# Twenty-four copies of memory values and four copies of keys: from VectorE to ScalarE

## The chip, the cores and the metric

The kernel runs on one core of one Trainium2 chip. The metric is the time of one execution on the device, in microseconds (us). Three runs of the kernel before gave 243.59, 243.83 and 243.85 us; their median is 243.83 us. Engines are named as in the profile: PE is TensorE, ACT is ScalarE, DVE is VectorE, POOL is GpSimd, SP is the queue that issues most stores and transposing DMAs.

## What is computed

The program is a chunked attention with a short context, followed by a gated feed-forward layer:

```python
# q, k, v: (4, 8, 768, 64); mem_k, mem_v: (4, 8, 8, 64)
for c in range(24):                       # chunks of 32 queries
    l, r = max(0, 32*c - 16), min(768, 32*c + 40)
    k_full = concat([mem_k, k[:, :, l:r]], axis=2)
    v_full = concat([mem_v, v[:, :, l:r]], axis=2)
    a = softmax(q[:, :, 32*c:32*c+32] @ k_full.T / 8)
    out[:, :, 32*c:32*c+32] = a @ v_full
x = out.transpose(0, 2, 1, 3).reshape(3072, 512)
y = (relu(x @ w_gate) * (x @ w_val)) @ w_out      # w_gate, w_val: 512x1536, w_out: 1536x512
```

Eight memory rows stand ahead of the context of every chunk, in the keys and in the values. They belong to a batch and a head, so all 24 chunks of a batch and head use the same eight rows.

## The kernel before

**Tiles and stages.** The 3072 rows are 24 tiles of 128 rows, six to a batch (`TPB`); a tile holds four chunks. For each tile `a` the attention stage runs: transposes of queries and keys, copies of them to `qT` and `kT`, `scores` (L283, into `s_ps`), `row_max` and `subtract` on DVE, `exponent` on ACT (three ACTIVATEs, L323), `row_sum`, `reciprocal` and `normalise` on DVE (`p_n`, L338), a transpose of the weights (`pT`, L344, by DMA from tile 14 on), then `values` (L354, 32 products into `xT_ps`, from tile 18 on `values_q`) and a copy to `xT`. The feed-forward stage works on blocks of 3, 3, 3, 4, 3, 4 and 4 tiles. For each of twelve column groups `m` PE makes `g_ps` and `v_ps` (four matmuls each, L407), ACT takes the relu of `g_ps` (L413), DVE multiplies it with `v_ps` (L419), and when all twelve are done, `second` (L428) makes `out_ps`, twelve matmuls for a tile, which ACT copies to `o_sb` (L90).

**Buffers that tie the engines together.** `g_ps`, `v_ps` and `out_ps` share four PSUM buffers (pool `fps`, L82). The transposes of queries, keys and weights and the results of `values` share two (`aps`, L84), and there is one for the scores (`sps`). The values lie in two sets `v_bd` (L106): a batch `b` uses set `b % 2`, so batch 2 writes over batch 0, and batch 3 over batch 1.

**The memory rows.** `mem_rows(b, par, hp, eng)` (L153 to L161) writes the eight memory rows of one head pair `hp` and one parity `par` to all 24 chunks of the set: 8 partitions of 24*64 = 1536 values, from an SBUF tile `vmem`, read with a step of 0 over the chunks. A batch takes eight such copies. Batch 0 gets its rows in another way (`pattern_spread`, L175), so there are 24 copies, for batches 1 to 3. `values` of the first tile of a batch needs all eight of its batch (L549).

**The memory keys.** `mem_keys(b, eng)` (L246) copies the keys of the memory to all chunks of `kT`: one copy of 128 partitions x 768 values for each batch. From tile 15 on, the keys are transposed by DMA to a tile `k_t` in SBUF, and `qk_copy` (L271) moves them into `kT`, 128 x 512 values.

**What sets the order.** The program writes its instructions in an order that a list scheduler in the kernel finds when the program is built (`schedule`, L673 to L781). Each operation is entered with `op(key, {engine: cost}, function, deps, prio, ...)`. An operation with two engines in its list goes to the one that is free first when it is ready: so do the copies of `pT`, `xT` and most of `qT` and `kT`. Whenever an engine falls free, the scheduler gives it the ready operation with the lowest `prio`: relu and gate have (0, ...), the copies to `o_sb` (0.5, ...), the attention stages of tile `a` (1, a, ...), the memory rows (1.5,), and `g_ps`, `v_ps` and `out_ps` on PE (2, ...). Nothing is interrupted once it has begun. On the chip each engine then runs its own list in that order. `holds_port` (L669) marks copies that, when DVE does them, the scheduler makes wait for POOL's current instruction; the marked ones are those of this change and a few others.

The rows of batch 1 may be copied once `vmem` has come and the scores of tile 6 have been started; those of batch 2 once `values` of tile 5 is done and the scores of tile 8 have been started; those of batch 3 after `values` of tile 11 and the scores of tile 14 (`MEM_LEAD`, L60 and L633). POOL issues the loads of queries, keys, values and weights in the order of `LOADS` (L63); SP issues stores and the transposing DMAs. Neither queue gets an instruction more or less by the change.

Of the kernel before, what the change touches and what calls it, by code (L numbers as in the profile page):

```python
# [15 lines left out]
ACT = mybir.ActivationFunctionType  # L16
# [4 lines left out]
def kernel(  # L21
# [12 lines left out]
    nc = tc.nc  # L34
# [53 lines left out]
    def copy(eng, o, i):  # L88
        if eng is nc.scalar:
            nc.scalar.copy(o, i)  # L90
        else:
            eng.tensor_copy(o, i)
# [60 lines left out]
    def mem_rows(b, par, hp, eng):  # L153
        p = slice(64 * par, 64 * par + NMEM)
        src = vmem[p, b, HP * par + hp]
        i = bass.AP(tensor=src.tensor, offset=src.offset, ap=[src.ap[0], [0, NCH], [1, D]])
        o = v_bd[b % NSET][p, hp, :, D * par:D * par + D]
        if eng is nc.sync:
            eng.dma_start(o, i)
        else:  # L160
            eng.tensor_copy(o, i)  # L161

    def pattern_load():
        for par in range(2):
# [56 lines left out]
    def pair_t(r, i):  # L221
        ps = TMP["pair", r, i] = aps.tile([128, 2, HP, 128], BF16, tag="aps", name="qk_ps")
        x = qk_b.pop(("pair", r, i))
        for j in range(2):
            for hp in range(HP):
                for r in range(2):
                    nc.tensor.transpose(ps[D * r:D * r + D, j, hp, :], x[:, 2 * hp + r, j, :], ident_b)  # L227

    def pair_q_copy(r, eng):
        b, t = divmod(2 * r, TPB)  # L230
        copy(eng, qT[b][:, :, 128 * t:128 * t + 256].rearrange("p h (s j) -> p j h s", j=2), TMP.pop(("pair", r, 0)))

    def pair_k_copy(r, j, eng):
        b, t = divmod(2 * r, TPB)
        ps = TMP["pair", r, 1]
        o = kT[b][:, :, 4 * t:4 * t + 8, :]
        copy(eng,
             bass.AP(tensor=o.tensor, offset=o.offset + j,
                     ap=[o.ap[0], [NCH * KW, HP], [KW, 8], [16 + NMEM, 2], [2, 8]]),
             ps[:, j].rearrange("p h (c x s) -> p h c x s", c=8, x=2))  # L240

    def new_batch(b):
        qT[b] = kvpool.tile([128, HP, S], BF16, name="qT")
        kT[b] = kvpool.tile([128, HP, NCH, KW], BF16, name="kT")

    def mem_keys(b, eng):  # L246
        src = kmemT[:, b]
        copy(
            eng, kT[b][:, :, :, 16:16 + NMEM],
            bass.AP(tensor=src.tensor, offset=src.offset,  # L250
                    ap=[src.ap[0], [NMEM, HP], [0, NCH], [1, NMEM]]))
# [4 lines left out]
    def qk_t(a, i):  # L256
        ps = TMP["qk", a, i] = aps.tile([128, HP, 128], BF16, tag="aps", name="qk_ps")
        x = qk_b.pop((a, i))
        for hp in range(HP):
            nc.tensor.transpose(ps[:, hp, :], x[:, 2 * hp:2 * hp + 2, :].rearrange("p h d -> p (h d)"), ident_b)  # L260

    def qk_dma(a, i):
        b, t = divmod(a, TPB)
        x = qk_b.pop((a, i)).rearrange("p h d -> p (h d)")
        if i == 0:
            o = qT[b][:, :, 128 * t:128 * t + 128]
        else:
            o = TMP["qk", a, i] = ktpool.tile([128, HP, 128], BF16, name="k_t")
        nc.sync.dma_start_transpose(o, x)

    def qk_copy(a, i, eng):  # L271
        b, t = divmod(a, TPB)
        ps = TMP.pop(("qk", a, i))
        if i == 0:
            copy(eng, qT[b][:, :, 128 * t:128 * t + 128], ps)
        else:
            o = kT[b][:, :, 4 * t:4 * t + 4, :]
            copy(eng,
                 bass.AP(tensor=o.tensor, offset=o.offset,
                         ap=[o.ap[0], [NCH * KW, HP], [KW, 4], [16 + NMEM, 2], [1, 16]]),  # L280
                 ps.rearrange("p h (c x s) -> p h c x s", c=4, x=2))
# [168 lines left out]
    def op(key, eng, fn, deps=(), prio=(0,), take=(), give=(), after=()):  # L450
        ops[key] = dict(eng=eng, fn=fn, deps=list(deps), prio=prio, take=list(take), give=list(give),
                        after=list(after))
# [4 lines left out]
    def psum(n):  # L457
        return {"ACT": 0.07 + 0.83e-3 * n, "DVE": 0.08 + 1.04e-3 * n}

    engine = {"ACT": nc.scalar, "DVE": nc.vector}  # L460
# [20 lines left out]
    for b in range(B):  # L481
        op(("kv", b), {"PE": 0.01}, lambda e, b=b: new_batch(b), take=["kv"],
           prio=(-5.5,) if b == 0 else (1, TPB * b - 2, 0), after=[("t", TPB * b - 2, 0)] if b else [])
        op(("new", b), {"DVE": 0.35, "ACT": 0.75}, lambda e, b=b: mem_keys(b, engine[e]), ["kmc", ("kv", b)],
           prio=(-4.5,) if b == 0 else (1, TPB * b - 2, 0))


    def pace(a):
        blk = block_of[a]
        if starts[blk] < TPB:  # L490
            return []
        m = NDC * (blk - 1) + NDC * (a - starts[blk]) // BLOCKS[blk] - LEAD[blk]
        return [("f", *divmod(max(m, 0), NDC), 0)]
# [4 lines left out]
    for a in range(NT):  # L498
        b, t = divmod(a, TPB)
        last = t == TPB - 1  # L500
        for i in (1, 0):
            if a < 2 * PAIRS:
                if a % 2:
                    continue
                op(("t", a, i), {"PE": 0.57}, lambda e, a=a, i=i: pair_t(a // 2, i), [("qk2", a // 2, i), "ib", ("kv", b)],
                   (1, a - i, 0), ["aps"], ["pr"], pace(max(a - i, 0)))
                if i:
                    for j in range(2):
                        op(("tc", a + j, i), {"ACT": 0.64, "DVE": 0.64}, lambda e, a=a, j=j: pair_k_copy(a // 2, j, engine[e]),
                           [("tc", a, i) if j else ("t", a, i)], (1, a - i, j), (), ["aps"] * j)  # L510
                else:
                    op(("tc", a, i), {"ACT": 1.2, "DVE": 1.22}, lambda e, a=a: pair_q_copy(a // 2, engine[e]), [("t", a, i)],
                       (1, a, 0), (), ["aps"])
            elif a < BY_DMA[i]:
                op(("t", a, i), {"PE": 0.24}, lambda e, a=a, i=i: qk_t(a, i), [("qk", a, i), "ib", ("kv", b)],
                   (1, a - i, 0), ["aps"], ["qk"], pace(max(a - i, 0)))
                op(("tc", a, i), psum(HP * 128), lambda e, a=a, i=i: qk_copy(a, i, engine[e]), [("t", a, i)],
                   (1, a - i, 0), (), ["aps"])
            else:
                op(("t", a, i), {"SP": 1.3}, lambda e, a=a, i=i: qk_dma(a, i), [("qk", a, i), ("kv", b)],  # L520
                   (1, a - i, 0), ["kt"] * i, ["qk"], [("p", a - i - 4)])
                if i:
                    op(("tc", a, i), {"ACT": 0.5, "DVE": 0.28}, lambda e, a=a, i=i: qk_copy(a, i, engine[e]),
                       [("t", a, i)], (1, a - i, 0), (), ["kt"], [("s", a - 2)] + pace(a - 1))
                else:
                    op(("tc", a, i), {"PE": 0.01}, lambda e: None, [("t", a, i)], (1, a - i, 0))
# [77 lines left out]
    def load_v_op(b, half, par, c0, c1, n, deps, after):  # L604
        for i, part in enumerate(reversed(v_parts(b, par, c0, c1))):
            rows = part[3] - part[2]
            load(("vl", b, half, n) if i == 0 else ("vx", b, n), rows * (part[5] - part[4]),
                 rows * (part[5] - part[4]) * 1.15e-3, lambda part=part: load_v_rows(*part), deps, (), after)
# [15 lines left out]
    def load_batch(b):  # L624
        deps = [("z", x) for x in range(HP)] if b < NSET else [("v", TPB * (b - NSET + 1) - 1)]
        for par in range(2):
            for hp in range(HP):
                if b <= MEM_BY_SP:
                    op(("mr", b, par, hp), {"SP": 0.73}, lambda e, b=b, par=par, hp=hp: mem_rows(b, par, hp, nc.sync),
                       deps + [(("vm", par), 0.2)], (0, par, hp))  # L630
                else:
                    op(("mr", b, par, hp), {"DVE": 0.48}, lambda e, b=b, par=par, hp=hp: mem_rows(b, par, hp, nc.vector),
                       deps + [("vm", par)], (1.5,), (), (), [("s", TPB * b - MEM_LEAD[b])])  # L633
        for par in range(2):
            load_v_op(b, 0, par, 0, HP * NCH, par, [], deps)
# [179 lines left out]
```

## Time and profile before

| | us |
|---|---|
| median of three runs | 243.83 |
| the profiled execution's own time | 244.88 |
| span of its records | 243.1 |
| PE busy | 228.5 |
| DVE busy | 146.4 |
| ACT busy | 114.7 |
| POOL busy | 77.9 |

The granted clock of TensorE is full in all 40 slices of the span. The span holds the records of the engines and their DMAs; 1.78 us of the profiled execution lie around it, and the profiled execution is 1.05 us above the median. The share of a row is an average over the whole span: the start (to about 27 us) has the first batch's attention, the stretch from 27 to 65 us has the products of the first two blocks, with attention of tiles 6 to 8 between them, from 65 to 86 us PE makes the `out_ps` of those two blocks, and from 86 us on block follows block. From 200 us on there is no attention left.

Matmuls of a chain overlap: four of `g_ps` for a three-tile block show 0.81 us, and the next chain of four begins 0.65 us after them.

### The profile page before, as it was taken

What the parts mean: (1) busy time and instruction counts of PE and PEld (TensorE: products, weight loads), DVE (VectorE), ACT (ScalarE), POOL (GpSimd) and SP (SyncE); (2) the same over time, 40 slices, a digit from 0 to 9 for tenths busy, and PEclk for the clock granted to TensorE, in tenths of its full rate; (3) what the DMA queues carried; (4) which work ended last, traced back from release to release, by engine and by line L of the source; (5) the groups of instructions that cost most, each with busy time, mean ns of one, the idle gap of its engine ahead of it and who ended that gap; (6) DMA issues with size and microseconds to landing.
All of it is one profiled execution on the core that took longest, in us unless ns stands there. A gap on an engine that the chain in (4) does not pass through costs nothing.

```text
span 243.1 us, 6045 instructions
## 1 busy us (share of the span) xinstructions
PE 228.5 (94%) x2521; PEld 123.7 (51%) x2521; DVE 146.4 (60%) x264; ACT 114.7 (47%) x239; POOL 77.9 (32%) x88
## 2 busy tenths in 40 slices
PE   0889899999997999999999999999999999999995
PEld 0667565655642565555444545665444444444443
DVE  5499963577899527984679428865258851143400
ACT  3658634556633365656545336554245532333212
POOL 8997899975347540428010000000000000000000
PEclk9999999999999999999999999999999999999999
DMA  6999999999999999989999332852421233200022
GB/s 65 175 153 173 166 164 181 199 187 171 147 138 214 201 175 135 139 71 101 124 196 117 65 108 71 128 103 51 131 67 22 27 61 110 88 2 0 0 81 94
DMA packets 114876, 27.97 MB, mean 115 GB/s; under 512 B 106016, under 2 KB 111904, under 8 KB 114848
## 3 DMA queue, kind: packets, MB, share of 16 engines
q0 software_dynamic: 91840, 16.61, 88.0%
q1 hardware_dynamic: 23008, 10.97, 21.0%
q8 instruction: 20, 0.33, 0.6%
q14 instruction: 8, 0.07, 0.1%
HBM read 33.24 MB, written 6.29 MB: 163 GB/s over the span
## 4 chain that ended last, share of the span: by engine, by line
PE 86%; DVE 8%; DMA 2%; ACT 1%; issue 1%; SPq 1%; ACTq 0%; DVEq 0%
PE g_ps L407 26%; PE v_ps L407 26%; PE out_ps L428 22%; PE qk_ps L227 3%; PE xT_ps L361 2%; DVE v_bd L161 2%; PE s_ps L295 2%; DMA kmem_f<-in_mem_k_dram 2%; PE pT_ps L344 1%; DVE p_n L338 1%; DVE sm L327 1%; DVE dif L315 1%; DVE mx L308 1%; PE idle_ps L399 1%; PE x_ps L371 1%
## 5 line engine op out<-in xcount | busy, mean ns | idle before, releaser
L419 DVE TENSOR_TENSOR gvT<-v_ps,g_relu 128x384 f16<-128x384 f32 (+1 forms) x84 | 51.4, 612 | 55.9 <-PE v_ps L407 55.0
L407 PE MATMUL g_ps<-xT,w_gate_sb 128*128 128x384 f16 (+1 forms) x336 | 76.2, 349 | 0.6 <-issue 0.5
L407 PE MATMUL v_ps<-xT,w_val_sb 128*128 128x384 f16 (+1 forms) x336 | 76.1, 349 | 0.0
L413 ACT ACTIVATE g_relu<-g_ps 128x384 f16<-128x384 f32 (+1 forms) x84 | 45.0, 536 | 58.9 <-PE g_ps L407 44.6
L428 PE MATMUL out_ps<-w_out_sb,gvT 128*128 128x512 f16 (+2 forms) x300 | 65.7, 371 | 0.0
L407 PEld LDWEIGHTS <-w_gate_sb 128*128 128x128 f16 x336 | 31.8, 98 | 28.7 <-issue 1.1
L407 PEld LDWEIGHTS <-w_val_sb 128*128 128x128 f16 x336 | 31.5, 98 | 27.6
L428 PEld LDWEIGHTS <-gvT 128*128 128x128 f16 x300 | 27.7, 98 | 29.8
L185 POOL DMA_DIRECT2D v_bd<-in_v_dram x24 | 27.4, 1150 | 9.7 <-issue 5.5
L90 ACT COPY o_sb<-out_ps 128x512 f32<-128x512 f32 (+2 forms) x25 | 14.2, 567 | 32.0 <-PE out_ps L428 29.9
L323 ACT ACTIVATE p_exp<-dif 128x64 f16<-128x64 f32 (+2 forms) x72 | 19.5, 335 | 11.1 <-DVE dif L315 10.9
L308 DVE TENSOR_REDUCE mx<-s_ps 128x8 f32<-128x512 f32 x24 | 16.4, 684 | 7.3 <-PE s_ps L295 7.0
L327 DVE TENSOR_REDUCE sm<-p_exp 128x8 f32<-128x512 f16 x24 | 16.3, 679 | 2.4 <-ACT p_exp L323 1.9
L338 DVE TENSOR_TENSOR p_n<-p_exp,rinv 128x512 f16<-128x512 f16 x24 | 16.5, 685 | 0.4
L315 DVE TENSOR_TENSOR dif<-s_ps,mx 128x512 f32<-128x512 f32 x24 | 16.3, 681 | 0.1
L161 DVE COPY v_bd<-vmem 8x1536 f16<-8x1536 f16 x24 | 15.7, 681 | 0.2
L207 POOL DMA_DIRECT2D qk_b<-in_q_dram x10 | 8.9, 888 | 14.8 <-DMA qT<-qk_b 7.2
L90 ACT CAST xT<-xT_ps 128x512 f16<-128x512 f32 x16 | 9.1, 584 | 8.1 <-PE xT_ps L361 8.1
L207 POOL DMA_DIRECT2D qk_b<-in_k_dram x10 | 9.0, 898 | 11.7 <-DMA qT<-qk_b 11.3
L361 PEld LDWEIGHTS <-v_bd 128*128 128x128 f16 x288 | 9.4, 96 | 3.2 <-issue 0.9
L361 PE MATMUL xT_ps<-pT,v_bd 128*128 128x32 f16 x288 | 9.7, 176 | 0.6 <-ACT xT L90 0.3
L227 PE MATMUL qk_ps<-ident_b,qk_p 128*64 128x128 bf16 x224 | 10.2, 242 | 0.0
(52 smaller groups left out, 138.5 us busy)
## 6 DMA issues: line engine op xcount, KB each, us to landing
out_dram<-o_sb SPq DMA_DIRECT2D x23, 256.0 KB, 2.4
v_bd<-in_v_dram POOLq DMA_DIRECT2D x5, 672.0 KB, 14.5
qk_p<-in_k_dram POOLq DMA_DIRECT2D x7, 256.0 KB, 7.7
qk_p<-in_q_dram POOLq DMA_DIRECT2D x7, 256.0 KB, 7.5
w_gate_sb<-in_moe_w_gate_dram POOLq DMA_DIRECT2D x8, 192.0 KB, 6.2
w_val_sb<-in_moe_w_val_dram POOLq DMA_DIRECT2D x8, 192.0 KB, 6.9
w_out_sb<-in_moe_w_out_dram POOLq DMA_DIRECT2D x2, 768.0 KB, 12.0
qk_b<-in_k_dram POOLq DMA_DIRECT2D x10, 128.0 KB, 10.5
```

The lines of the kernel that those rows point to most:

```text
L90: nc.scalar.copy(o, i)
L161: eng.tensor_copy(o, i)
L185: nc.gpsimd.dma_start(dst[64 * par + NMEM + s0:64 * par + NMEM + s1, c0:c1, D * par:D * par + D], bass.AP(tensor=v.tensor, offset=v[b, HP ...
L308: nc.vector.reduce_max(SM[a, "mx"], s4, axis=AX.X)
L315: nc.vector.tensor_tensor(out=SM[a, "dif"].rearrange("p (m r) a s -> p r m a s", r=2), in0=S_ps.pop(a).rearrange("p r (m a) s -> p r m a s ...
L323: nc.scalar.activation(p[:, :, :, s0:s0 + k1 - k0], dif[:, :, :, k0:k1], ACT.Exp, scale=SCALE)
L338: nc.vector.tensor_tensor(out=P_n[a], in0=SM.pop((a, "p")), in1=rinv_b, op=ALU.mult)
L361: nc.tensor.matmul(ps[:, hp, r], lhsT=v_bd[b % NSET][:, hp, 4 * t + g, :], rhs=x[:, hp, r], start=True, stop=True)
L407: nc.tensor.matmul(ps, lhsT=w[:, f, 128 * m:128 * m + 128], rhs=xTs[blk][:, f, :], start=(f == 0), stop=(f == NFC - 1))
L413: nc.scalar.activation(st["r", m], st.pop((0, m)), ACT.Relu)
L419: nc.vector.tensor_tensor(out=st["gv"][:, m, :], in0=st.pop((1, m)), in1=st.pop(("r", m)), op=ALU.mult)
L428: nc.tensor.matmul(st["o", t, cols], lhsT=st["gv"][:, m, 128 * t:128 * t + 128], rhs=w_out_sb[:, m, slice(*cols)], start=(m == 0), stop=(m ...
```

## The change

The memory rows of batches 1 to 3, the memory keys of all batches and the copies of `k_t` are given to ACT alone. The scheduler's costs for them become 1.35 for the rows (0.48 on DVE before), 0.75 for the memory keys and 0.5 for `k_t`. Priorities, dependencies and buffers stay. In the trace of before, ACT already made the memory keys of batches 0 and 3 and seven of the nine copies of `k_t`.

```diff
@@ mem_rows
         if eng is nc.sync:
             eng.dma_start(o, i)
         else:
-            eng.tensor_copy(o, i)
+            copy(eng, o, i)
@@ for b in range(B)
-        op(("new", b), {"DVE": 0.35, "ACT": 0.75}, lambda e, b=b: mem_keys(b, engine[e]), ["kmc", ("kv", b)],
+        op(("new", b), {"ACT": 0.75}, lambda e, b=b: mem_keys(b, engine[e]), ["kmc", ("kv", b)],
@@ keys that were transposed by DMA
-                    op(("tc", a, i), {"ACT": 0.5, "DVE": 0.28}, lambda e, a=a, i=i: qk_copy(a, i, engine[e]),
+                    op(("tc", a, i), {"ACT": 0.5}, lambda e, a=a, i=i: qk_copy(a, i, engine[e]),
@@ load_batch
-                    op(("mr", b, par, hp), {"DVE": 0.48}, lambda e, b=b, par=par, hp=hp: mem_rows(b, par, hp, nc.vector),
+                    op(("mr", b, par, hp), {"ACT": 1.35}, lambda e, b=b, par=par, hp=hp: mem_rows(b, par, hp, nc.scalar),
                        deps + [("vm", par)], (1.5,), (), (), [("s", TPB * b - MEM_LEAD[b])])
```

`copy` (L88) calls `nc.scalar.copy` for ACT and `tensor_copy` for the other engines.

## The prediction, made before the change was run

> **What bounds the kernel now.** First the table of busy time by stretches, then the chain of waits, then the rows of the operations. Of the 19 stretches of ten microseconds from 40 to 230 us, PE is busy throughout in all but one, 70 to 80 us (7.81 of 10). Here are five shorter stretches around it; the first number after the length is PE's busy time, the third DVE's, the fourth ACT's:
>
> ```profile
> 60.00:65.00 5.00, 5.00 (x89) 3.21 (x87) 3.94 (x9) 3.56 (x8) 0.89 (x1) 1.00 2.42 146
> 65.00:70.00 5.00, 5.00 (x59) 2.36 (x56) 4.90 (x8) 2.73 (x6) 3.50 (x4) 1.00 3.06 132
> 70.00:75.00 5.00, 4.72 (x26) 2.10 (x25) 4.87 (x9) 1.71 (x5) 2.35 (x3) 1.00 2.33 188
> 75.00:80.00 5.00, 3.09 (x18) 1.34 (x17) 4.91 (x9) 1.28 (x3) 2.46 (x2) 1.00 1.89 215
> 80.00:85.00 5.00, 5.00 (x63) 2.84 (x62) 2.46 (x6) 1.83 (x4) 3.16 (x2) 1.00 2.12 190
> ```
>
> PE lacks 0.28 and 1.91 us here while DVE is full (4.87 and 4.91 of 5) and ACT mostly idle. The chain of waits says why. It leaves PE at 65.9 us and comes back to it through DVE:
>
> ```profile
> 74.69 0.59 ACT o_sb L90
> 75.28 0.68 DVE sm L327
> 75.96 0.03 issue
> 75.99 1.86 DVE v_bd L161
> 77.86 0.02 issue
> 77.88 0.20 DVE rinv L331
> 78.08 0.41 DVE v_bd L161
> 78.49 0.61 DVE p_n L338
> 79.10 0.05 issue
> 79.15 0.40 PE pT_ps L344 x4
> ```
>
> One copy of memory rows (L161) stands between the sum and the reciprocal of tile 9. PE's list has the transpose of that tile's weights (L344) ahead of 18 more products of `out_ps`, so PE waits for the normalised weights. The timeline shows why that copy took so long, and how long PE stood idle (in brackets):
>
> ```profile
> 75.26 2.20 POOL L185 DMA_DIRECT2D v_bd<-in_v_dram  x1
> 75.99 1.85 DVE L161 COPY v_bd<-vmem 8x1536 f16<-8x1536 f16 x1
> ...
> 79.15 0.40 PE L344 MATMUL pT_ps<-ident_h,p_n 128*128 128x128 f16 x4 [1.91 <-DVE p_n L338]
> ```
>
> The median copy is 0.544 us (view of the tile `v_bd`); this one took 1.85 and ended 0.38 us after POOL's instruction did. The 16 copies of batches 1 and 2 took 11.40 us of DVE between 60 and 85 us, where 16 x 0.544 would be 8.70.
>
> **The change, part by part.**
>
> *What goes.* The 24 copies leave DVE (15.7 us of busy time). Between 65 and 82 us this takes the copy of 1.85 us and its neighbours out of the chain; without them, reciprocal and normalisation of tile 9 follow the sum at 75.97 directly. The rest of the softmax moves up likewise. I take out both idle pieces: **-2.19 us** (0.28 + 1.91). What is late next in that stretch is the filler itself: PE has 72 products of `out_ps` there, and these need only `gvT` and free PSUM buffers.
>
> The Trainium skill (SBUF — State Buffer, "Who interferes with whom") says that a VectorE instruction in a mode that uses two ports and a GpSimd instruction exclude each other for a whole instruction, whichever began first. The row of 1.85 us under a POOL instruction agrees. By that rule alone the removal is worth the excess, 1.85 - 0.54 = 1.31, and the time would be 0.88 us higher than in my sum; the chain above shows that the whole copy goes, not the excess alone.
>
> *What the copies cost on ACT.* The trace has no such copy on ACT. The nearest rows are copies from SBUF to SBUF:
>
> ```profile
> L90 ACT COPY kT<-k_t 128x512 bf16<-128x512 bf16 x7 | 4.3, 614 | 0.0
> L90 ACT COPY kT<-kmemT 128x768 bf16<-128x768 bf16 x2 | 1.7, 832 | 0.0
> L90 ACT CAST vmem<-vmem_f 8x256 f16<-8x256 f32 x1 | 0.4, 403 | 0.1
> ```
>
> From 256 to 768 values the time grows by 429 ns, 0.838 ns each; that the small one has 8 partitions, as the new copies have, shows that partitions do not matter. So 1536 values give 832 + 768 x 0.838 = 1475 ns, my estimate. Bounds: 0.54 us (it runs as on DVE) and 1.66 us (two of 832 ns). 24 x 1.475 = 35.4 us go onto ACT, whose busy time rises from 114.7 to about 151 us with the smaller copies. Neighbours that do not wait overlap: the two `kT` copies at 65.14 take 1.33 us together though one takes 0.73, so some 0.1 us of each is hidden.
>
> *Are they ready in time?* This is the step that decides. `values` of tile 6 (L361, at 83.27 us) needs all eight copies of batch 1; without the idle time PE would come there at 81.08. From 65.1 to 83.3 us ACT is busy 6.48 us; 8 x 1.475 = 11.80 makes 18.28 us of work, in 16.0 us. But some 15 back-to-back pairs save 0.1 each (-1.5), and one `kT` copy (0.73) and the `pT` copy (0.59) may run on DVE by their operation's list, as DVE is freed (-1.3): 15.5 us. The copies stand last in priority, so they fill every gap, but each holds up what comes behind it by up to 1.4 us. Behind `values` the four `xT` copies (0.58 on ACT, 0.69 on DVE) can meet the first copies of batch 2. PE has filler, the last six products of `out_ps` (1.3 us). I take a loss between nothing and one copy (1.475) and choose **+0.6 us**.
>
> *Batch 2's copies among the relus (84 to 96 us).* A three-tile pair `g_ps`, `v_ps` takes PE 1.30 us. The relu at 88.31 starts 0.84 us after its `g_ps` (87.47) and ends at 88.80; with four PSUM buffers that buffer is wanted two pairs later, at 90.07: 1.27 us of slack. A copy just started holds the relu for up to 1.4 us. One relu fits between two copies, so the delay builds up and two or three of the eight cost 0.1 to 0.2: **+0.3 us**. If every relu were held fully and PE had no slack, 8 x (1.475 + 0.49 - 1.30) = 5.3 us; that is the other end.
>
> *Batch 3's copies (116 to 137 us).* Here blocks have four tiles: the relu at 118.51 ends at 119.11 and its buffer is wanted at 117.38 + 4 x 0.86 = 120.82, slack 1.71 us, more than one copy. ACT is busy 10.03 of 20.8 us; 11.8 more does not quite fit, but the rows are needed only by tile 18, behind 156 us. **0**; up to 1 if copies and exponents fall together (10.03 + 11.80 - 20.8).
>
> *The small copies.* Two memory-key copies go from 0.36 us on DVE to 0.83 on ACT, two `k_t` copies from 0.28 to 0.61. The first stands at 19.88 us, where DVE is busy 9.77 us in the ten from 20 us; taking it out may give 0.38 us, and putting it ahead of an exponent may cost 0.83. I take **0**. The others are covered by PE's products; uncovered they cost 2 x 0.33 + 0.47 = 1.1. POOL and SP get no other instructions; POOL no longer waits for these copies (it stood idle 4.38 us before 81.84 on "issue"), so loads of later tiles can come earlier: **0**, the chain has no wait for a load after 7 us.
>
> *The sum.* Span 243.1 - 2.19 + 0.6 + 0.3 = 241.8; own time 244.88 - 1.29 = 243.6. The profiled execution is 1.05 us above the median, so the median becomes 243.83 - 1.29 = **242.5 us**.
>
> **The rivals.**
>
> *A, the forecast* (chance 0.45): 241.7 to 243.3. For it: ACT is idle for 64% of the time from 65.1 to 83.3 us, and DVE is the chain there.
>
> *B, ACT becomes the bound: slower* (0.24). The eight copies of batch 1 are not done when the filler is used up, and behind them the `xT` copies of tiles 6 to 8 each meet a copy of batch 2. Price: 18.3 us of ACT work from 65.1 ends at 83.4, 1.0 us behind 81.08 + 1.3; two `xT` copies held by 1.475 each are 2.95; with relus 0.3 to 1.0, together 4.2 to 5.0, less 2.19: 245.9, at most 246.6. It decides against the change once waits of PE between 80 and 96 us exceed 2.19. For it: the ledger above has a margin of only 0.5 us. Against: the `xT` copies can go to DVE. The Trainium skill (ScalarE: Activation LUTs, "Rules for kernel authors") advises VectorE over ScalarE for simple elementwise work, up to about three times faster per element; 1.475 to 0.544 is 2.7 and agrees, and this rival is what that advice would make here.
>
> *C, the wait moves* (0.18): the idle 2.19 us go, and about as much comes back at tile 6's `values` and the relus: 243.4 to 244.3, 243.8 in the middle.
>
> *D, all of it and the start too* (0.13): -2.19 and -0.38, nothing new: 241.3 to 241.7.
>
> That the change does not do what it says I give no chance of its own: the lists name one engine. But the scheduler orders everything anew, which is in the widths.
>
> A measurement of this kernel can tell 0.2% (0.5 us) from no change. Faster: A and D, 0.58; same: C, 0.18; slower: B, 0.24. The range reaches from D's lower end to 245.5, which leaves out B's upper half: 241.3 to 245.5. The copy's bounds move little of it: at 0.54 us the forecast is A's or D's lower end, at 1.66 the ledger grows by 1.5 us and leads to C.
>
> **What would show it.** Right: the copies in ACT's list at 1.4 to 1.5 us each; DVE's busy time near 130 us, ACT's near 150; no wait for `p_n` of 1.91 us at L344; PE starts block 2's `g_ps` (86.17 now) between 84 and 85.5 us. Wrong: a wait of L361 for an ACT copy of `v_bd` or `xT` that exceeds 2 us, relus that start over 2 us behind their `g_ps` with PE idle in front of the next, or a first `g_ps` (26.83 now) later by half a microsecond.

## The result: 1.3% slower, and the profile after

Four executions of the changed kernel took 245.91 to 247.87 us, median **246.82**; four of the kernel before took 243.59 to 243.85, median 243.81. The ratio is 1.0127, 95% interval 1.0083 to 1.0171. The forecast was 242.5 and the range ended at 245.5; the time lies beyond it, on the side of rival B. Measured again (e7, below), the same kernel gave 246.36 against 243.88, 1.0098 (1.0070 to 1.0125).

Much of the forecast came about. The copies are on ACT at the estimated price (1464 ns, estimate 1475). The row of the page, with busy time and mean ns at its end:

```profile
L90 ACT COPY v_bd<-vmem 8x1536 f16<-8x1536 f16 x24 | 34.9, 1464 | 0.3
```

The idle time of PE between 70 and 80 us is gone. The table of busy time by stretches, PE's first, then PEld, DVE and ACT:

```profile
70.00:75.00 5.00, 5.00 (x28) 2.40 (x27) 3.57 (x7) 5.00 (x9) 3.38 (x4) 1.00 2.38 164
75.00:80.00 5.00, 5.00 (x28) 2.37 (x27) 0.42 (x1) 4.88 (x6) 1.46 (x1) 1.00 1.85 222
80.00:85.00 5.00, 4.96 (x80) 3.10 (x78) 1.77 (x3) 4.95 (x5) 4.88 (x4) 1.00 2.00 208
```

PE is full where it lacked 0.28 and 1.91 us, and ACT, not DVE, is the full engine beside it. In PE's timeline the transpose that had waited 1.91 us starts without a wait, and so does `values` of tile 6; block 2's first product waits 0.30 us for a copy that DVE now makes:

```profile
75.78 0.39 PE L344 MATMUL pT_ps<-ident_h,p_n 128*128 128x128 f16 x4
...
82.47 0.95 PE L361 MATMUL xT_ps<-pT,v_bd 128*128 128x32 f16 x32
...
85.26 0.81 PE L407 MATMUL g_ps<-xT,w_gate_sb 128*128 128x384 f16 x4 [0.30 <-DVE xT L92]
```

The chain of waits changes hands a little later. From 80.7 to 97.2 us it runs through ACT; an excerpt:

```profile
93.14 1.47 ACT v_bd L90
94.60 0.02 issue
94.63 0.49 ACT g_relu L413
...
95.14 1.47 ACT v_bd L90
96.61 0.02 issue
96.64 0.50 ACT g_relu L413
97.14 0.04 issue
97.18 0.81 PE v_ps L407 x4
```

A copy of memory rows, the relu that stood behind it, the next copy: a period of 2.00 us (93.14 to 95.14), where PE needs 1.30 us for a pair of products. Not all of the 0.70 us is lost each time, since PE has scores and transposes of the attention to make between the pairs. The same stretch by busy time, before:

```profile
85.00:90.00 5.00, 5.00 (x66) 3.15 (x62) 1.38 (x3) 3.03 (x6) 1.92 (x3) 1.00 2.14 171
90.00:95.00 5.00, 5.00 (x79) 2.86 (x73) 2.84 (x5) 2.86 (x5) 0.88 (x1) 1.00 1.97 146
95.00:100.00 5.00, 5.00 (x80) 3.03 (x76) 4.40 (x11) 2.68 (x8) 0.99 (x2) 1.00 1.97 138
```

and after:

```profile
85.00:90.00 5.00, 4.59 (x40) 2.65 (x40) 1.47 (x4) 4.98 (x7) 0.16 (x1) 1.00 2.20 179
90.00:95.00 5.00, 4.62 (x70) 2.52 (x68) 4.04 (x6) 4.90 (x6) 0.71 (x1) 1.00 2.72 139
95.00:100.00 5.00, 4.77 (x64) 2.82 (x66) 4.46 (x11) 4.90 (x10) 1.22 (x2) 1.00 2.47 123
```

ACT goes from 8.57 to 14.78 busy of 15 us, and PE is no longer full.

To see where the time went I cut the span at the starts of a few products in PE's timeline. All values are us of the profiled execution; "rows" are the memory rows, and the rest of the table is used in the next section.

| kernel | first `g_ps` at | to first `out_ps` | to block 2's `g_ps` | block 2's products | its `out_ps` | block 3 to block 4 |
|---|---|---|---|---|---|---|
| before | 26.83 | 38.86 | 20.48 | 19.72 | 9.77 | 33.59 |
| after | 27.16 | 39.63 | 18.47 | 21.22 | 10.18 | 34.12 |
| after, again (e7) | 27.84 | 39.63 | 18.47 | 21.21 | 10.19 | 34.20 |
| keys alone (e1) | 26.82 | 39.35 | 19.38 | 19.72 | 9.77 | 33.60 |
| rows alone (e2) | 26.76 | 38.46 | 18.46 | 21.22 | 10.18 | 34.21 |
| rows of batch 1 alone (e3) | 26.80 | 38.72 | 18.50 | 19.73 | 9.76 | 33.60 |
| all but batch 2's rows (e4) | 26.91 | 39.85 | 17.93 | 19.73 | 9.76 | 34.52 |
| short copies (e5) | 26.58 | 39.63 | 18.47 | 19.62 | 9.76 | 33.66 |
| rows as a maximum on DVE (e6) | 26.57 | 38.36 | 20.56 | 19.73 | 9.76 | 33.60 |
| before, no idle products after 20 us (e11) | 27.09 | 39.55 | 18.75 | 19.73 | 9.76 | 33.60 |
| rows of batch 1 alone, again (e12) | 27.68 | 38.45 | 17.94 | 19.72 | 9.77 | 33.60 |
| all, fewer instructions at the start (e13) | 27.00 | 38.41 | 18.47 | 21.22 | 10.18 | 36.43 |
| batch 1's rows, fewer at the start (e14) | 27.11 | 38.19 | 17.93 | 19.72 | 9.77 | 33.59 |
| all, halves (e15) | 27.47 | 38.58 | 18.73 | 20.97 | 9.76 | 37.40 |
| all, quarters (e16) | 27.35 | 39.90 | 18.47 | 20.70 | 10.74 | 35.69 |
| all but batch 3's rows (e17) | 27.37 | 39.56 | 18.46 | 21.23 | 10.18 | 34.01 |

After less before: +0.33 + 0.77 at the start, -2.01 in the stretch of the forecast, +1.50 in block 2's products, +0.41 in its `out_ps`, +0.53 in block 3: +1.53 us. The two profiled executions differ by 246.44 - 244.88 = 1.56, so the stages account for it. The medians differ by 3.01, because the execution profiled before lay 1.07 above its median and the one after 0.38 below.

One stage shows how much an execution can differ. In e11 (an edit at the start of the kernel before, told below), which has DVE's instructions of this stretch in the order of the kernel before, the stretch of the forecast took 18.75 us in place of 20.48:

```profile
74.49 2.20 POOL L185 DMA_DIRECT2D v_bd<-in_v_dram  x1
...
76.09 0.99 DVE L161 COPY v_bd<-vmem 8x1536 f16<-8x1536 f16 x1
...
78.38 0.40 PE L344 MATMUL pT_ps<-ident_h,p_n 128*128 128x128 f16 x4 [0.64 <-DVE p_n L338]
```

The copy that took 1.85 us before takes 0.99 here, since POOL's instruction began 1.60 us ahead of it and not 0.73; both copies end 0.4 us after POOL's instruction. PE waits 0.64 us, and not 1.91. So the 2.01 us of this stage are those of two single executions; other executions of the kernel before may have had less to lose.

### The profile page after: what moved, and what is told of

Read it like the earlier page. It is cut to its first block, busy times and chain, and to the rows that moved or that the text cites. A ratio compares the mean times of both kernels' runs of the same rounds, so it can differ in the third digit from the quotient of the medians.

```text
span 244.6 us, 6055 instructions
## 1 busy us (share of the span) xinstructions
PE 228.7 (94%) x2526; PEld 123.8 (51%) x2526; DVE 137.4 (56%) x242; ACT 145.0 (59%) x261; POOL 77.7 (32%) x88
## 4 chain that ended last, share of the span: by engine, by line
PE 78%; ACT 9%; DVE 4%; issue 3%; DMA 3%; POOL 2%; ACTq 0%; POOLq 0%
PE out_ps L428 24%; PE v_ps L407 23%; PE g_ps L407 23%; ACT v_bd L90 6%; DMA qk_p<-in_q_dram 3%; PE xT_ps L361 2%; PE qk_ps L227 2%; ACT g_relu L413 2%; PE s_ps L295 2%; POOL qk_p L216 2%; PE pT_ps L344 1%; DVE dif L315 1%; PE x_ps L371 1%; DVE p_n L338 1%; DVE mx L308 1%
## 5 line engine op out<-in xcount | busy, mean ns | idle before, releaser
L90 ACT COPY v_bd<-vmem 8x1536 f16<-8x1536 f16 x24 | 34.9, 1464 | 0.3
L92 DVE CAST xT<-xT_ps 128x512 f16<-128x512 f32 x8 | 5.3, 682 | 8.0 <-PE xT_ps L361 8.0
(50 smaller groups left out, 145.0 us busy)
```

## The experiments

**Theory M:** the copies' own time on ACT, among the relus, costs what the removed stall brings, and more. **Rivals:** the new order of the other instructions costs it; or the keys do. A later theory, **I**, concerns the start: PE waits there for its instructions. The expectations use these letters, and say what others mean.

### The parts of the change, one by one

*e1: the keys alone.* In the change, rows as before:

```diff
-            copy(eng, o, i)
+            eng.tensor_copy(o, i)
-        op(("mr", b, par, hp), {"ACT": 1.35}, ... mem_rows(b, par, hp, nc.scalar)
+        op(("mr", b, par, hp), {"DVE": 0.48}, ... mem_rows(b, par, hp, nc.vector)
-        op(("tc", a, i), {"ACT": 0.5}, ...
+        op(("tc", a, i), {"ACT": 0.5, "DVE": 0.28}, ...
```

(The two copies of `k_t` keep their choice of engine here; only the memory keys are bound to ACT.)

> Only the memory keys go to ScalarE; memory rows and k_t copies stay as before. Theory M (the 3.0 us are made of four pieces: +1.1 us in the start, where the memory-key copy of batch 1 on ScalarE reorders the first batch's attention; -2.0 between 65 and 86 us; +1.9 between 86 and 116 us, where batch 2's row copies hold up the relus of block 2; +0.6 between 116 and 150 us): the start's piece alone, 244.3 to 244.9 us, first g_ps at 27.1 to 27.2 us instead of 26.8. Rival L (the loss is ScalarE's load by the rows, and the late start of the changed kernel's profile is chance): 243.6 to 244.0, first g_ps at 26.8 us.

Measured: 244.27 against 244.0, ratio 1.0025 (1.0004 to 1.0047), just under the range of theory M. The first `g_ps` comes at 26.82, as rival L had it, and not at 27.1; it is the stretch from the first product to the first `out_ps` that grows, by 0.49. The stall for `p_n` stays, 1.27 us.

*e2: the rows alone.*

```diff
-        op(("new", b), {"ACT": 0.75}, ...
+        op(("new", b), {"DVE": 0.35, "ACT": 0.75}, ...
-        op(("tc", a, i), {"ACT": 0.5}, ...
+        op(("tc", a, i), {"ACT": 0.5, "DVE": 0.28}, ...
```

> Only the 24 row copies go to ScalarE; keys and k_t copies as before. Theory M: no late start, so -2.0 + 1.9 + 0.6, 244.0 to 244.8 us. Rival L: the whole loss stays, 246 to 247 us.

Measured: 245.19 against 244.0, ratio 1.0044 (1.0017 to 1.0070). This lies between the range of theory M (244.0 to 244.8) and that of L. The stages are those of the change from block 2's first product on, and those of before (or 0.4 less) at the start. So in the profiles the longer start goes with the keys, and the rest with the rows. The medians do not add up like this: the whole change in e7 costs 2.48 us, the rows alone 1.19 and the memory keys alone 0.27. About 1.0 us is left for the copies of `k_t`, which no run moves alone, or for the parts together; this stays open.

*e3: batch 1's rows alone*, as e2, and

```diff
-        op(("mr", b, par, hp), {"ACT": 1.35}, ... nc.scalar)
+        op(("mr", b, par, hp), {"ACT": 1.35} if b == 1 else {"DVE": 0.48}, ... engine[e])
```

> Only the eight row copies of batch 1 go to ScalarE; those of batches 2 and 3, the keys and k_t as before. Theory M: the gain of the stretch from 65 to 86 us without its price, 241.6 to 242.2 us, no idle piece of 1.9 us ahead of the transpose of tile 9's weights. Rival D (VectorE's copies of batch 2 then move into the same stretch and keep it full): 243.3 to 244.0. Rival L: ScalarE full from 66 to 82 us costs something by itself, 243.8 or more.

Measured: **242.7** against 244.0, ratio 0.9942 (0.9913 to 0.9972); measured again on another chip (e12, below), 242.52 against 244.05, 0.9934 (0.9910 to 0.9957). The forecast's gain is real when only the copies that cause it are moved: 1.98 us in its stretch of the profiled executions, 1.30 and 1.53 us by the medians, so the times lie above theory M's 241.6 to 242.2. By the medians of e2 and e3, the rows of batches 2 and 3 cost 245.19 - 242.70 = 2.49 us; by their stages 1.49 + 0.42 + 0.61 = 2.52.

*e4: all but batch 2's rows.*

```diff
-        op(("mr", b, par, hp), {"ACT": 1.35}, ... nc.scalar)
+        op(("mr", b, par, hp), {"ACT": 1.35} if b != 2 else {"DVE": 0.48}, ... engine[e])
```

> The whole change, but batch 2's row copies stay on VectorE. Theory M: without the 1.9 us of held relus in block 2, 244.6 to 245.2 us; relus of block 2 start under 1.2 us behind their g_ps. Rival L (any ScalarE load costs alike; a third of the copies gone takes a third of the loss): 245.6 to 246.0 us. If batch 2's copies do not matter: 246.8.

Measured: 244.91 against 244.0, ratio 1.0025 (0.9998 to 1.0052). Block 2's products are back at 19.73 and its `out_ps` at 9.76; both excesses were batch 2's copies.

### Is it the copies' time, or the order?

*e5: the change, with copies of batches 2 and 3 that take little time.* The order of all instructions is that of the change; the copies write 2 of the 24 chunks, and the kernel leaves the memory rows of the others out.

```diff
-        i = bass.AP(tensor=src.tensor, offset=src.offset, ap=[src.ap[0], [0, NCH], [1, D]])
-        o = v_bd[b % NSET][p, hp, :, D * par:D * par + D]
+        i = bass.AP(tensor=src.tensor, offset=src.offset, ap=[src.ap[0], [0, NCH if b < 2 else 2], [1, D]])
+        o = v_bd[b % NSET][p, hp, 0:NCH if b < 2 else 2, D * par:D * par + D]
```

> The whole change with every instruction in the same order, but the row copies of batches 2 and 3 write 2 of the 24 chunks, so that 22 of 24 chunks of those batches lack their memory rows; each copy should take some 0.3 us instead of 1.46. Read by stages, from the first g_ps of a block to its first out_ps and on. Theory M (the time of the copies on ScalarE holds the relus): block 2's products take 19.7 us as in the kernel before (21.2 in the changed kernel), and first g_ps of block 3 to first g_ps of block 4 33.6 us (34.1 in the changed kernel); late start unchanged. Rival O (the new order on PE, with scores and transposes at other places, costs it): 21.2 and 34.1 stay.

One execution took 243.28 us, though its stretch up to the first `out_ps` is as long as the change's (39.63). The view of the tile `v_bd` (ns: least, median, most) shows the short copies:

```profile
L90 ACT COPY v_bd<-vmem x24: 279/293/1467, 66.3 to 132.9; 8x128 f16<-8x128 f16 x16, 8x1536 f16<-8x1536 f16 x8
```

and by stretches PE is full and ACT is not:

```profile
85.00:90.00 5.00, 5.00 (x45) 3.03 (x43) 2.64 (x5) 2.77 (x6) 0.19 (x1) 1.00 2.02 203
90.00:95.00 5.00, 5.00 (x108) 3.01 (x107) 4.05 (x9) 3.48 (x9) 0.88 (x1) 1.00 2.64 89
```

With the same order, block 2's products take 19.62 us, its `out_ps` 9.76 and block 3 33.66. The order is not the cause; the time on ACT is, and M holds for 1.60 + 0.42 + 0.46 us of the change.

*e15 and e16: the same work in shorter pieces.* What makes this time cost? A copy that has begun may hold a relu (then shorter copies help), or ACT may have no time for the work (then they do not). Each copy of batches 2 and 3 becomes two instructions (e16: four):

```diff
+                    n = 2 if b > 1 else 1
+                    for k in range(n):
-                    op(("mr", b, par, hp), {"ACT": 1.35}, ... mem_rows(b, par, hp, nc.scalar)
+                        op(("mr", b, par, hp, k), {"ACT": {1: 1.35, 2: 0.75, 4: 0.43}[n]}, ... mem_rows(b, par, hp, nc.scalar, k, n)
```

> The whole change, but each copy of memory rows of batches 2 and 3 is made by two instructions of 768 values (12 chunks each) instead of one of 1536; batch 1's copies, engines, priorities and buffers stay as in the change. Two readings of what the eight copies of a batch cost among the relus. Holding (H): a copy that has begun can't be interrupted, so it holds a relu that comes ready behind it; the work itself would fit. A half takes about 0.83 us (the 768-value row of the copy of the memory keys), less than the 1.27 us of slack that the four PSUM buffers give a relu, so block 2's products, 21.2 us in the change and 19.7 before, come back to 19.7 to 20.2, and the stretch from block 3's first product to block 4's from 34.1 to about 33.7: 2.0 us less in all, 244.4 us. Work (W): ACT has no time for the copies, 4.9 of 5 us busy from 85 to 100 us. Halves are more work on ACT (16 x 0.83 = 13.3 us a batch against 8 x 1.464 = 11.7), so block 2's products stay at 21.2 or grow towards 22, and the time is 246.4 or more.

> As the halves, but four instructions of 384 values (6 chunks) for each copy of memory rows of batches 2 and 3. By the row of 256 values (0.40 us) and 0.84 ns for each further value a quarter takes 0.51 us, 16.3 us a batch. Holding (H): a relu is held by at most 0.5 us, so block 2's products are at 19.7 and the time at 244.2 or below, even with 4.6 us more work for ACT in a batch than in the change. Work (W): the products of block 2 grow beyond the change's 21.2, to 22 or more, and the time is above 247.

Measured: halves 246.76 against 243.99, ratio 1.0118 (1.0078 to 1.0159); quarters 247.73 against 243.99, 1.0147 (1.0124 to 1.0169). Neither reading gets all of it. In block 2 both are right in part: a half takes 0.83 us, the relus up to 97 us hold PE no more, and the products shrink by 0.25 (quarters 0.52) of the 1.50. Behind them, `out_ps` gets back the 0.41 with halves, but grows by another 0.56 with quarters, and halves start block 2 0.26 us later. In all, from the first `out_ps` to block 3, halves bring 0.41 us and quarters cost 0.04. ACT, which in the change has air again from 100 us on (4.43 of 5 in the five from there), is now almost full to 105, and what waits there is the attention. Halves, by stretches and in PE's timeline:

```profile
100.00:105.00 5.00, 4.13 (x73) 2.63 (x71) 4.70 (x10) 4.84 (x10) 0.00 (x0) 1.00 1.88 131
```

```profile
103.17 0.55 PE L362 MATMUL xT_ps<-pT,v_bd 128*128 128x32 f16 x16 [0.87 <-ACT pT L90]
```

So shorter copies bring back a sixth to a third of what the products lost, and the work that ACT has no room for comes out behind them; the times go with W (both also have the wait for keys told below). That W is the rest is argued from ACT's busy time, not shown apart. The Trainium skill (Perfetto Trace Analysis, "Optimizing Scalar/DVE Operations") says that where ScalarE or VectorE is not saturated but causes bubbles on other engines, breaking up instructions may let work finish sooner. Its condition is the point: here ACT was busy 14.78 of 15 us, and the pieces brought no time.

*e17: all but batch 3's rows*, as e4 with `b != 3`.

> The whole change, but batch 3's eight copies of memory rows stay on DVE; those of batches 1 and 2 and all keys are on ACT as in the change. Theory M (the copies' time on ACT among the relus costs, and moves SP's transposes of keys behind those of the weights, so that ACT stands before a k_t that has not landed in some executions): without batch 3's copies the stretch from block 3's first product to block 4's is 33.6 instead of 34.1 us and ACT waits for no k_t; block 2's products stay at 21.2 and the start is that of the change. Time 246.4 - 0.5 = 245.9 or, if waits for k_t are in many executions of the change, down to 245; its executions lie closer together than the change's 245.4 to 247.9. If batch 3's copies cost nothing in most executions (my prediction's 0), the time stays at 246.4 or above.

Measured: 245.65 against 243.87, ratio 1.0075 (1.0051 to 1.0098); e7 gave 1.0098. Block 3 takes 34.01 us, where I expected 33.6. Its products take 22.09 (22.56 in the change, 22.10 with short copies), so the 0.46 of batch 3's copies goes; but in the new order its `out_ps` takes 11.92 (11.56 in the change), which gives 0.36 back. What those copies cost over many executions is not settled by this run. The executions spread over 244.64 to 246.79, no less than those of e7 (245.44 to 247.18).

### A wait that only some profiles show

The profiles of e13, e15 and e16 are above 35 us in block 3. ACT's timeline of e13 shows what makes most of it:

```profile
134.63 0.62 ACT L90 COPY kT<-k_t 128x512 bf16<-128x512 bf16 x1 [2.33 <-DMA k_t<-qk_b]
```

and in PE's timeline the scores stand behind it:

```profile
135.30 0.30 PE L295 MATMUL s_ps<-kT,qT 64*32 64x64 bf16 x26 [1.75 <-ACT kT L90]
```

ACT waits for transposed keys, and the relus stand behind ACT. In e15 and e16 these waits of ACT are 2.36 and 1.66 us, those of PE 1.85 and 1.04. In the profile of the change the same copy found its keys at 133.70, 5.3 us after SP issued the transfer (128.37). In the kernel before, SP issued it at 121.02 and DVE copied at 138.35, 17 us later. In e13 it was issued at 127.01 and landed 7.6 us later. The change brings SP no instruction, but its order puts the transposes of weights and queries ahead of this one, and a lead that a slow landing eats up. How many executions it hits the runs do not show: only the profiled ones have a timeline.

### Was it the port?

*e6: rows on DVE, as the maximum of a row with itself*, in the kernel before:

```diff
-            eng.tensor_copy(o, i)
+            eng.tensor_tensor(out=o, in0=i, in1=i, op=ALU.max)
```

> The kernel before in the same order, but the row copies on VectorE are made as the maximum of the row with itself, a two-source instruction. Theory P (the long copies of before waited for GpSimd's instructions because a one-source copy in a fast mode needs a port that GpSimd holds): every copy takes about the same, 0.9 to 1.0 us by the rows of 512-wide 16-bit two-source instructions (0.69) scaled, none near 1.85 behind GpSimd's 2.2 us instruction; the stretch from the first out_ps to block 2's first g_ps is then 20 to 21 us, since eight slower copies give back what the waits cost. Rival Q (any VectorE instruction waits there): copies up to 2.2 us remain and the stretch grows past 22 us.

One execution took 244.28 us. The view of `v_bd`:

```profile
L161 DVE TENSOR_TENSOR v_bd<-vmem x24: 895/941/951, 64.6 to 134.4; 8x1536 f16<-8x1536 f16 x24
```

No instruction of this form waits for POOL, one at 75.82 under POOL's 74.51 to 76.71 included: the excess of the 1.85 us of before was that wait. But every copy now takes 0.94 in place of 0.54, PE waits 0.96 + 1.32 us for `p_n`, and the stretch is 20.56 us (20.48 before). What had to go from DVE was the copies, not the excess alone, as the forecast had it.

### Again, and a later start of batch 2's copies

*e7: the change once more*, no edit.

> The changed kernel once more, beside the others on this chip. Theory M: by its stages 1.5 us above before, 245.3 to 246.9 us; PE waits on issue twice between 20 and 30 us, at the same instructions as in all other runs, 1.4 to 2.0 us together (0.7 in the profile of before). Rival L: 246.8 or more with the same stages, the rest outside the stages.

Measured: 246.36 against 243.88, 1.0098 (1.0070 to 1.0125), with the stages of the first profile within 0.1 from the first product to block 4; the first product itself was 0.68 later.

*e8: e3 with batch 2's copies, on DVE, let in two tiles later.*

```diff
-    MEM_LEAD = (0,0,4,4)
+    MEM_LEAD = (0,0,2,4)
```

> Rows of batch 1 on ScalarE as in the kernel with only batch 1 moved, and batch 2's rows on VectorE held back until the scores of tile 10 have been started (about 90 us). Theory M: the stretch to block 2's first g_ps falls from 18.5 to about 18.0 us, since VectorE has no copies left there, block 2's products stay at 19.7; 242.2 us (241.6 to 242.7). Rival D: VectorE's copies in block 2 hold up the gates and give it back, 242.7 to 243.5.

Measured: 244.0 against 243.88, 1.0012 (0.9988 to 1.0036), a miss, above both expected ranges. The copies end late: `values` of tile 12 waits 1.31 us for DVE's at 114.66, and block 2's `out_ps` takes 11.06 in place of 9.76.

### The start

In 12 of the 14 profiles with all idle products PE halts on "issue", waiting for nothing that the profile shows, after its matmul 348, and in nine of them again after its matmul 475. The profiles of e6 and e15 have neither halt, so the halts are not in every profile, though the expectation of e9 says so. PE's timeline before:

```profile
22.58 0.30 PE L361 MATMUL xT_ps<-pT,v_bd 128*128 128x32 f16 x6 [0.20 <-issue]
...
29.12 0.48 PE L407 MATMUL g_ps<-xT,w_gate_sb 128*128 128x384 f16 x2 [0.50 <-issue]
```

After:

```profile
23.26 0.23 PE L361 MATMUL xT_ps<-pT,v_bd 128*128 128x32 f16 x3 [0.89 <-issue]
...
29.41 0.65 PE L407 MATMUL v_ps<-xT,w_val_sb 128*128 128x384 f16 x3 [1.05 <-issue]
```

The two halts end 6.2 to 6.5 us apart in both kernels, and the DMA queue named "instruction" moves two packets of 16 KB between 20 and 30 us, while the DMA engines are full. So PE may wait for its instructions. With the memory keys of batch 1 on ACT (22.75 us, 0.81 long) the first batch's attention is reordered, the normalised weights of tile 2 come at 24.13 where it was 22.92, and the scheduler fills PE with 117 idle products (L399, ahead of the first product) where it was 112. Theory I: these reach the limit sooner, and fewer of them bring the time back.

*e9, e10, e11: no idle products after 20 us*, in the change, in e3 and in the kernel before:

```diff
-  if o is None and e == "PE" and "ident" in done and 6.0 < t and ("f", 0, 0, 0) not in started:
+  if o is None and e == "PE" and "ident" in done and 6.0 < t < 20.0 and ("f", 0, 0, 0) not in started:
```

> The whole change, but the idle products that PE makes while it waits for work are left out after 20 us of the scheduler's clock (44 of 117). Theory I (in every profile PE stops on issue ahead of its matmuls number 349 and 476 counted from the start, 5.9 to 6.5 us apart where the second stop shows; the reordered start puts more idle products between the two, so PE reaches the second one too early and with less real work done): no wait on issue near 28 us, first g_ps to first out_ps 38.4 to 38.8 us instead of 39.6, 0.8 to 1.1 us less than the changed kernel. Rival C (PE runs slower without the idle products, or the waits depend on time alone): first chains of g_ps longer than 0.65 us, no gain.

> Rows of batch 1 alone on ScalarE, and the idle products left out after 20 us as in the kernel before this. Theory I: first g_ps to first out_ps 38.4 instead of 38.7 us, 0 to 0.4 us faster than with batch 1's rows alone, 242.2 to 242.7 us. Rival C: 242.7 or more.

> The kernel before with the idle products left out after 20 us. Theory I: first g_ps to first out_ps 38.4 instead of 38.9 us, 0 to 0.5 us faster than before, 243.3 to 243.9 us. Rival C: as before or slower.

Measured: the change 249.2 against 244.05, 1.0192 (1.0141 to 1.0243); e3 243.51, 0.9991 (0.9963 to 1.0019); before 244.93, 1.0056 (1.0028 to 1.0083). All are slower than with the idle products. The halt near 29 us is gone, but something else came; by stretches of e9, the third number from the end is the granted clock:

```profile
20.00:25.00 5.00, 2.16 (x73) 1.78 (x73) 4.96 (x11) 3.01 (x9) 3.10 (x5) 0.93 1.27 186
25.00:30.00 5.00, 4.33 (x64) 2.45 (x63) 3.30 (x7) 2.38 (x6) 4.03 (x7) 0.50 2.00 162
```

It was 1.00 in both with the idle products. At 0.50 the first chains of four start 1.25 us apart in place of 0.65. These runs say nothing on theory I; they show what the idle products are for.

*e13, e14: every second idle product, twice as wide*, in the change and in e3: half as many instructions for about the same time, all else in the same order.

```diff
-        if "idle" not in TMP:
-            TMP["idle"] = fps.tile([128, 128], F32, tag="fps", name="idle_ps")
-        nc.tensor.matmul(TMP["idle"], lhsT=ident_h, rhs=ident_h, start=True, stop=True)
+        TMP["idle"] = TMP.get("idle") or [0, fps.tile([128, 2, 128], F32, tag="fps", name="idle_ps")]
+        TMP["idle"][0], wide = TMP["idle"][0] + 1, [ident_h.ap[0], [0, 2], [1, 128]]
+        TMP["idle"][0] % 2 and nc.tensor.matmul(TMP["idle"][1], lhsT=ident_h, rhs=bass.AP(tensor=ident_h.tensor, offset=ident_h.offset, ap=wide), start=True, stop=True)
```

*e12* is e3 again, measured beside e9 to e11.

> Rows of batch 1 alone on ScalarE once more, for the interval: 242.2 to 243.0 us, ratio 0.992 to 0.997. If its first measurement was chance: 243.5 to 244.2.

> The whole change with every other instruction in its order, but half as many idle products, each 256 wide instead of 128, so that PE is kept as busy with fewer instructions. Theory I (the late start of the changed kernel is half a wait of PE for its own instructions, at fixed counts of instructions, which the idle products bring nearer): the granted clock stays at 1.0, no wait on issue near 28 us, first g_ps to first out_ps 38.5 to 38.9 us instead of 39.6; 0.7 to 1.2 us less than the changed kernel, 244.9 to 245.7 us. Rival T (the waits come at a time, not at a count): 39.4 to 39.9 us there, 246.3 us.

> Rows of batch 1 alone on ScalarE, and half as many idle products of double width. Theory I: clock 1.0, no wait on issue near 28 us, first g_ps to first out_ps 38.4 us instead of 38.7; 241.9 to 242.5 us. Rival T: 242.5 to 242.8 us, as with batch 1's rows alone.

Measured: the change 245.93 against 244.11, 1.0073 (1.0047 to 1.0100); e3 **241.79** against 244.11, 0.9899 (0.9858 to 0.9939), the best of all. The clock stays at 1.00, PE has no halt on "issue" near 23 or 29 us, and the stretch from first product to first `out_ps` falls from 39.63 to 38.41 in the change and from 38.45 (e12) to 38.19 in e3. The change's time lies above theory I's range, e3's just below it. So theory I holds as far as these go: half the idle instructions, and the halts and 1.2 us of the change's stretch are gone. Two things keep it from being settled. The profiles of e15 and e6, with all their 117 and 112 idle products, have no halt either, and e12 lacks the second halt that e3, the same kernel, has; so halts come and go between executions. And the times fell by 0.25 and 0.35%, about as much as their intervals are wide. That the cause is the loading of instructions is argued from the fixed counts and the queue, not shown.

What the halts cost can be read without a theory. The second lies in the stretch from the first product to the first `out_ps`. Without it, what is left of the stretch is 38.34 to 38.48 us in the six profiles with batch 1's memory keys on DVE and all idle products, and 38.57 or 38.58 in the eight with these keys on ACT. So 0.55 of the change's 0.77 is a longer halt (1.05 for 0.50) and 0.22 the order. The halt was there in two of those six profiles and in seven of those eight, up to 1.33 us in e16; why the keys bring it is open. The first halt costs the change little: where it is missing (e13, e15), PE waits 0.87 and 0.89 us for the normalised weights of tile 2 instead.

## Why the prediction was wrong, point by point

- **The stall, -2.19: right for the profiled execution; for the median it may be too large.** The wait is gone and the stretch is 2.01 us shorter; PE's next wait there is 0.30 for `xT`. But the size was read from one execution, 1.05 us above the median, and the sum carried that distance over to the changed kernel, whose profiled execution lay 0.38 below its own. The stall changes with when POOL's instruction falls: 0.64 us in e11 and 1.27 in e1. Over many executions e3 gained 1.30 and 1.53 us.
- **The copy, 1475 ns: right** (1464). Two copies in a row take 2.85 us, so the 0.1 of overlap is there; between a copy and the relu that waits behind it (93.14 + 1.47, relu at 94.63) it is not.
- **"Are they ready in time?", +0.6: pessimistic.** The eight copies of batch 1 end at 82.41, `values` of tile 6 starts at 82.47, and PE had products of `out_ps` until then. DVE took eight `xT` copies and three of 128 x 1024 for `qT` (two and one before), as the ledger allowed for some; that is why DVE is at 137.4 us and not at 130, and ACT at 145.0 and not at 150.
- **"Batch 2's copies among the relus", +0.3: this step failed.** It measured +1.50 in the products and +0.41 behind them. I looked at one relu and its slack of 1.27 us, and made no ledger of the stretch as I had for batches 1 and 3. It stands in the rows of before: ACT busy 8.57 of 15 us from 85 to 100, plus 8 x 1.46 = 11.7, is 20.3, and 17.4 with the six copies that came after the first two. The slack of the buffers lasts for two pairs (it was even larger than I said: with the transposes between, that buffer was wanted at 90.74, 1.94 us after its relu), then ACT's copy plus relu sets when a buffer comes free. My other end, 5.3, counted eight held relus; two of the eight copies had ended (85.9) before the first relu came.
- **"Batch 3's copies", 0 to 1:** +0.53 in the profile, 0.46 of it by e5; and a risk that I had not seen. "POOL and SP get no other instructions" is true of their number, but SP's order changed, and with it the lead of the transposed keys.
- **"The small copies", 0: wrong by 1.10**, the start. I weighed 0.38 of DVE against 0.83 of ACT. Of the 0.77 behind the first `g_ps`, 0.55 is a longer halt of PE on "issue" and 0.22 the reordering of the first batch. The kernel before shows the halts (0.20 and 0.50), and I passed over these rows. I had named "a first `g_ps` later by half a microsecond" as what would speak against the forecast; it was 0.33 late, which says little: e3 and e12, the same kernel, have it at 26.80 and 27.68.
- **Rival B** had the direction and about the size (245.9, at most 246.6), from the wrong place: tile 6's `values` and `xT`, which were in time. ACT did become the bound, one stage later; that the number fits is luck.

The sum: forecast -1.29, measured +1.53 in the profiled executions. The 2.82 between them are 1.61 of batch 2 (1.91 less 0.3), 1.10 of the start and 0.53 of batch 3, less 0.42 that the first stretch did better (-2.01 for -2.19 + 0.6). The other half of the 3.0 us between the medians is 1.07 + 0.38, where the two profiled executions lay about their medians. Its cause stays open. Candidates are a stall that was longer in the profile of before than in most executions (0.64 in e11), the late first product of e7 (0.68) and the late keys of e13, e15 and e16.

## What to carry to other kernels

A stall by one engine's copies pays for moving those copies, not all of their kind: the same copy gained 0.25 us apiece (1.98 of e3's profile by eight; 0.16 to 0.19 by the medians) where ACT idled, and cost 0.24 apiece (1.91 by eight) where ACT was serving PE's buffers. Make the ledger (busy time of the receiving engine in that stretch, plus what comes) for every stretch in which copies land, since slack of a single instruction does not tell what a row of eight does. A stall that hangs on when two engines meet has another length in each execution, so its price needs more than one profile. And where a list scheduler finds the order, read the new order of every queue, also of those that get no instruction.

## What was not expected of the hardware

- PE halts on "issue" after 348 and after 475 matmuls, whatever these are, for 0.2 to 1.3 us, in most profiles; in the two with half as many idle instructions in front it does not, nor in e6 and e15 with all of them.
- The granted clock fell to 0.64 within 24 to 25 us of e9 and to 0.50 from 25 on, though PE's longest idle time there was 1.73 us; from 22 to 26 us PE was busy about 1.2 of 4 us. The Trainium skill (TensorE: Matmul & The Clock Gate, "Part 1: The HAM clock gate") has half clock after an idle window of about 3.4 us; the half rate agrees, but here a thinly filled window was enough, with no gap of that length.
- A transposing transfer of 128 x 512 keys had landed 5.3 us after its issue in the profile of the change, and took 7.6 to 8.7 us in those of e13, e15 and e16, which issue it in the same order.
- A copy on DVE that began under an instruction of POOL ended 0.4 us after that instruction, in before, e1 and e11 (1.85, 2.07 and 0.99 us long); the same work as a maximum of two inputs took 0.95 us under it.
